# Softmax sums corrected on VectorE, weight sums in two jobs and weight conversion in another order, in a fused attention and two-layer MoE kernel

## The chip, the cores and the metric

One core of one Trainium2 chip. The metric is the device time of one execution in microseconds (us); the kernel before was timed three times and the median counts.

## The reference, cut to what matters

```python
attn = exp(scores - max);  attn = attn / (sum(attn) + 1e-09);  x = attn @ v     # window of 128, B=2, H=8, S=576, D=64
p = domain_probs / (domain_probs.sum(-1) + 1e-09)
for e in range(4):  out += p[:, e] * (relu(x @ w1[e]) @ w2[e])                  # x 1152x512, w1 512x1024
h = out @ w_in;  g = h * cos(h);  return g @ w_out                              # w_in 512x2048, in float64 words
```

## The kernel before

Every product of the two MoE stages is made in three TensorE passes over operands split into a high and a low part. The high part is a ScalarE (ACT) copy, the low part a subtraction on GpSimd (POOL) or VectorE (DVE). All subtractions are recorded under the helper's line, L130, so they are told apart by tile: `w1t` and `w2t` are split weights, `sm` sums of weight blocks, `xs` and `xq` split activations, `h` and `hpair` split hidden values.

The program order is written by hand. Each engine works through its own list in that order, and SyncE (SP) does the same with the DMAs it issues.

**Attention** (0 to 94 us) runs over 20 steps k, two for each block of queries, four heads in one step. Step k makes the scores and exponentials of k, the sums and reciprocals of step k-1 (`att_sums`), one weight job, the transposes of step k-3, the normalisation of step k-1 on POOL (`att_normalise`) and the product with v of step k-4 (after which `split_x` or `transformed` splits the result, ACT first and DVE behind it):

```python
at(k, att_scores); at(k - 1, att_sums); fill(k, 0)
at(k - LAG, att_transpose); at(k - 1, att_normalise); fill(k, 1)
at(k - LAG - 1, att_pv); fill(k, 2)
```

From k = 4 each `fill(k, 0)` takes one job from the generator `weights()`. A job is half a split (an ACT cast and a POOL subtraction), or the four POOL sums of `first_sums` in one go.

**Groups 0 to 7** (`early`) are the ReLU MoE, 512 hidden columns each; groups 8 to 11 are the cosine layer, whose weights `convert` makes from float64 words while groups 0 to 6 run (32 conversions of five stages, `cv`). A group is a list of steps made by `steps(g)`: two calls of `pair` (seven products over `xs`), `layer2(g, t)` for nine row tiles t (product over `h` for t < 3, over `hpair` otherwise) and `plain(g + 1, q)` (P0 to P3, a product of the next group over `xq`). `run` does for each step: the matmuls, then `advance` (one stage of every open cosine chain), the step's jobs, its `cv` stages, `move(2)` (two stages of a transform), and last the step's own evacuation. Group 7 (`turn`) also transposes the MoE's result by `flip(t)`, written f1 to f8, and builds the new operands `xs`.

The hidden values of a cosine group go through a chain of ACT, DVE, ACT, DVE, ACT, POOL, whose last instruction writes the low part in `hpair`.

Of the kernel before, what the change touches and what calls it, by code (L numbers as in the profile page):

```python
# [49 lines left out]
def tile_kernel(ctx, tc, qT, kT, v, probs, w1, w2, w_in, w_out, out):  # L50
    nc = tc.nc
# [96 lines left out]
    def weights():  # L148


        def two_parts(eng, hi, lo, src):
            n = src.shape[1] // 2
            for p in range(2):
                s = slice(p * n, (p + 1) * n)
                nc.scalar.activation(out=hi[:, s], in_=src[:, s], func=AF.Copy)  # L155
                sub(eng, lo[:, s], src[:, s], hi[:, s].bitcast(F32))
                yield

        raws = {}

        def first(g, j):
            raw = raws[j] = raw_t.pop((1, g, j))
            w = w_t[1, g, j] = w1p.tile([128, 2, 2, 1024], F32R, name="w1t", tag="w1t")
            yield from two_parts(nc.gpsimd, w[:, 0, 0], w[:, 1, 0], raw.rearrange("p m f -> p (m f)"))

        def first_sums(g, j):

            raw, w = raws[j], w_t[1, g, j]
            a11, a12 = raw[:, 0:2, 0:128], raw[:, 2:4, 0:128]
            a21, a22 = raw[:, 0:2, 128:256], raw[:, 2:4, 128:256]  # L170
            sm = ssp.tile([128, 4, 2, 128], F32, name="sm", tag="sm")
            nc.gpsimd.tensor_tensor(out=sm[:, 0], in0=a21, in1=a22, op=ALU.add)
            sub(nc.gpsimd, sm[:, 1], sm[:, 0], a11)
            sub(nc.gpsimd, sm[:, 2], a11, a21)
            sub(nc.gpsimd, sm[:, 3], a12, sm[:, 1])
            loads_ahead()
            yield
            yield from two_parts(nc.gpsimd, w[:, 0, 1], w[:, 1, 1], sm.rearrange("p s m f -> p (s m f)"))

        def second(g, j):  # L180
            raw = raw_t.pop((2, g, j))
            w = w_t[2, g, j] = w2p.tile([128, 2, 2, DM], F32R, name="w2t", tag="w2t")
            for f in range(2):
                nc.scalar.activation(out=w[:, 0, f], in_=raw[:, f], func=AF.Copy)  # L184
                sub(nc.gpsimd, w[:, 1, f], raw[:, f], w[:, 0, f].bitcast(F32))
                if f:
                    loads_ahead()
                yield

        for g in range(NG1 + NG2):  # L190
            for todo, j in order_of(g):
                yield from {"raw": first, "sums": first_sums, "second": second}[todo](g, j)
# [60 lines left out]
    def converts():  # L253

        gens = [convert(k) for k in range(32)]
        next(gens[0])
        for k, c in enumerate(gens):
            if k + 1 < len(gens):
                next(gens[k + 1])
            yield from c  # L260
# [72 lines left out]

    state, xps = {}, {}

    def att_scores(u, g):
        b, i = u
        s0, n = UNITS[i]
# [10 lines left out]
                )  # L349
        p = ppool.tile([128, 4, 256], F32, name="p", tag="p")  # L350
        nmax = stp.tile([128, 4], F32, name="nmax", tag="nmax")
        den = stp.tile([128, 4], F32, name="den", tag="den")
        rec = stp.tile([128, 4], F32, name="rec", tag="rec")
        for m in range(2):
            for hh in range(2):
                k = 2 * m + hh
                h = 4 * g + k
                nc.vector.tensor_tensor_reduce(  # L358
                    out=p[:n, k, :wid], in0=ps[hh][:n, m, :wid], in1=bm[:n, h, c0 : c0 + wid],
                    scale=-0.125, scalar=3.0e38, op0=ALU.add, op1=ALU.min,  # L360
                    accum_out=nmax[:n, k : k + 1],
                )
                nc.scalar.activation(  # L363
                    out=p[:n, k, :wid], in_=p[:n, k, :wid], func=AF.Exp, scale=-1.0,
                    bias=nmax[:n, k : k + 1], accum_out=den[:n, k : k + 1],
                )
        state[u, g] = p, den, rec, wid

    def att_sums(u, g):
        n = UNITS[u[1]][1]  # L370
        p, den, rec, wid = state[u, g]
        nc.gpsimd.tensor_scalar(out=den[:n], in0=den[:n], scalar1=1e-9, scalar2=None, op0=ALU.add)
        nc.vector.reciprocal(out=rec[:n], in_=den[:n])  # L373

    def att_normalise(u, g):
        n = UNITS[u[1]][1]
        p, den, rec, wid = state[u, g]
        for s in (slice(0, 2), slice(2, 4)):
            nc.gpsimd.tensor_tensor(  # L379
                out=p[:n, s, :wid], in0=p[:n, s, :wid],  # L380
                in1=rec[:n, s].unsqueeze(2).to_broadcast([n, 2, wid]), op=ALU.mult,
            )
        state[u, g] = p

# [293 lines left out]
    with tc.manual_schedule():  # L678

        warm = ppool.tile([128, 4, 256], F32, name="warm", tag="p")  # L680
        nc.vector.memset(warm[:, 0], 0.0)
        for _ in range(WARM):
            nc.tensor.matmul(
                ps1.tile([128, 512], F32, name="o_ps", tag="o_ps")[:, :256],
                warm[:, 0, :128], warm[:, 0], start=True, stop=True,
            )
# [4 lines left out]
        def fill(k, s):  # L691
# [4 lines left out]
                nc.sync.dma_start(out=pr, in_=probs.rearrange("(t p) e -> p t e", p=128))  # L696
            if (k, s) == (11, 0):
                routing()
            if s == 0 and 4 <= k < 18:
                next(jobs)  # L700
            if s == 1 and 12 <= k < 20:
                q, half = divmod(k - 12, 2)
# [23 lines left out]
    def steps(g):  # L726
# [15 lines left out]
            if turn and j == 0:  # L742
                yield flip(0), 0, 0, 0
        if g > 0:
            yield layer2(g, 1), 2, 2 * turn, 2
            yield layer2(g, 2), 2, 2 if turn else int(not last), 2
        order = (
            ("f1", 3, "f2", 6, "f3", "P0", "f6", 4, "P1", 7, "f4", 5, "f7", 8, "f5", "P2", "f8", "P3") if turn else
            ("P0", 6, 3, "P1", 7, 4, "P2", 8, "P3", 5)
        )  # L750
        njobs = 0 if last else 2 if turn else 5 if early else 9
        if g == 0:
            njobs += 1
        for k, o in enumerate(order):
            more = min(njobs, 2 if g == 0 and k == 0 else 1)
            if isinstance(o, int):
                assert not any(c > 0 for c, _ in chains)
                yield layer2(g, o), 2, more, 2 if k in (1, 4, 7) else 1 if k < 9 else 0
            elif o[0] == "f":
                yield flip(int(o[1])), 0, 0, 0  # L760
                continue
            elif not last:
                yield plain(g + 1, int(o[1])), 2, more, 2
            njobs -= more

    def run(groups):
        for g in groups:
            for step, stages, njobs, ncv in steps(g):
                next(step)
                for _ in range(stages):  # L770
                    advance()
                for _ in range(njobs):
                    next(jobs)
                for _ in range(ncv):
                    next(cv, None)
                move(2)
                next(step, None)
            while moved:
                move(24)
# [2 lines left out]
    hpair = hpp.tile([128, 2, NFG, PAIR], F32R, name="hpair")  # L782
    cv = converts()
    with tc.manual_schedule():
        run(range(NG1 - 1))
        left = sum(1 for _ in cv)
        assert not left, left
# [43 lines left out]
```

## Time and profile before

| | |
|---|---|
| Time, median of 3 (lowest, highest) | 676.09 us (674.96, 679.61) |
| The profiled execution: time, span of its instructions | 675.06 us, 673.3 us |
| TensorE busy (matmul, weight load) | 648.1 us, 569.5 us |
| VectorE, ScalarE, GpSimd busy | 420.4, 336.7, 372.4 us |

The span is the time from the first instruction to the last; the execution's own time is 1.8 us longer. Busy times of engines overlap. TensorE's idle time is in three places: the attention, the passage from group 0 to group 1 (130 to 146 us) and the turn (460 to 500 us). Between them the profile shows it busy without a break for 10-us slices on end.

### The profile page before, as it was taken

The numbers are of one execution on the slowest core, as the hardware profiler recorded it, in microseconds if no ns is written. First come the engines' busy times: TensorE is split into PE (matmuls) and PEld (weight loads), VectorE is DVE, ScalarE is ACT, GpSimd is POOL, SyncE is SP. The second block draws the span as 40 slices with busy tenths as digits, with TensorE's granted clock in tenths as the row PEclk, the third lists the DMA queues.
The fourth block names the chain that finished last, engine by engine and source line by source line (L and its number), as shares of the span: only waits on it lengthen the run. The fifth ranks groups of instructions, "written<-read, shape, count | busy, mean of one in ns | idle before, by whom it ended". The sixth has DMA issues, their size and how long they took to land.

```text
span 673.3 us, 9797 instructions
## 1 busy us (share of the span) xinstructions
PE 648.1 (96%) x3516; PEld 569.5 (85%) x3516; DVE 420.4 (62%) x821; ACT 336.7 (50%) x768; POOL 372.4 (55%) x376
## 2 busy tenths in 40 slices
PE   8879999979999999999999999999899999999997
PEld 5667789878898898998998998988788998998976
DVE  5645674587866858659669663455675464564562
ACT  6868744245334334344343251246675675675660
POOL 3987737517538147357166174194458749649540
PEclk7989999999999999999999999999999999999999
DMA  8135101553625504526325322011001200201002
GB/s 259 40 121 164 32 1 34 183 159 87 198 76 156 173 32 156 173 57 207 104 102 202 126 48 78 32 63 33 1 32 33 77 17 32 93 2 47 34 31 93
DMA packets 39728, 60.41 MB, mean 90 GB/s; under 512 B 5632, under 2 KB 22016, under 8 KB 39680
## 3 DMA queue, kind: packets, MB, share of 16 engines
q1 hardware_dynamic: 39680, 59.80, 27.7%
q8 instruction: 27, 0.44, 0.3%
q14 instruction: 21, 0.17, 0.1%
HBM read 49.04 MB, written 10.75 MB: 89 GB/s over the span
## 4 chain that ended last, share of the span: by engine, by line
PE 75%; DVE 8%; ACT 6%; POOL 5%; issue 3%; DMA 2%; SPq 0%; ACTq 0%; DVEq 0%; POOLq 0%
PE o_ps L627 38%; PE o_ps L533 20%; PE o_ps L561 13%; POOL p L379 2%; DVE u L505 2%; ACT r L503 2%; PE s_ps L346 2%; DMA cr<-w_in 2%; ACT u L502 2%; PE x_ps L429 2%; POOL hpair L130 1%; PE t_ps L401 1%; DVE o_ps L576 1%; DVE u L511 1%; DVE c L576 1%
## 5 line engine op out<-in xcount | busy, mean ns | idle before, releaser
L627 PE MATMUL o_ps<-w2t,hpair 128*128 128x512 f32 x864 | 207.2, 392 | 1.2 <-POOL hpair L130 1.0
L627 PEld LDWEIGHTS o_ps<-w2t,hpair 128*128 128x128 f32 x864 | 160.7, 188 | 35.1 <-POOL hpair L130 2.3
L533 PE MATMUL o_ps<-xs,w1t 128*128 128x384 f32 x1008 | 182.3, 336 | 8.3 <-ACT p L582 3.0
L533 PEld LDWEIGHTS o_ps<-xs,w1t 128*128 128x128 f32 x1008 | 175.4, 188 | 13.7 <-ACT p L582 3.9
L130 POOL TENSOR_TENSOR w1t<-raw,w1t 128x512 fp32r<-128x512 f32 x48 | 66.1, 1390 | 95.3 <-ACT w1t L155 95.2
L130 POOL TENSOR_TENSOR w2t<-raw,w2t 128x512 fp32r<-128x512 f32 x48 | 62.4, 1312 | 90.0 <-ACT w2t L184 88.7
L561 PE MATMUL o_ps<-xq,w1t 128*128 128x384 f32 x576 | 110.3, 338 | 0.0
L561 PEld LDWEIGHTS o_ps<-xq,w1t 128*128 128x128 f32 x576 | 101.6, 188 | 3.3
L627 PE MATMUL o_ps<-w2t,h 128*128 128x512 f32 x432 | 103.3, 392 | 0.0
L627 PEld LDWEIGHTS o_ps<-w2t,h 128*128 128x128 f32 x432 | 80.5, 188 | 16.1 <-issue 0.2
L505 DVE SCALAR_TENSOR_TENSOR u<-r,u 128x384 f32<-128x384 f32 x48 | 38.7, 810 | 57.8 <-ACT r L503 57.8
L130 POOL TENSOR_TENSOR w1t<-sm,w1t 128x512 fp32r<-128x512 f32 x48 | 67.2, 1416 | 7.4 <-ACT w1t L155 7.3
L130 POOL TENSOR_TENSOR hpair<-u,hpair 128x384 fp32r<-128x384 f32 x32 | 32.6, 1039 | 42.5 <-ACT hpair L513 42.5
L155 ACT ACTIVATE w1t<-sm 128x512 fp32r<-128x512 f32 x48 | 30.3, 631 | 45.7 <-POOL sm L130 45.7
L521 DVE SCALAR_TENSOR_TENSOR hpair<-o_ps,hpair 128x384 fp32r<-128x384 f32 x48 | 26.7, 556 | 33.1 <-ACT hpair L520 33.1
L363 ACT ACTIVATE p<-p,nmax 128x256 f32<-128x256 f32 (+2 forms) x80 | 36.3, 455 | 17.0 <-DVE nmax L358 17.0
L232 ACT ACTIVATE cr<-cr 128x512 int32<-128x512 uint32 x32 | 21.6, 675 | 44.6 <-DMA cr<-w_in 30.9
L520 ACT ACTIVATE hpair<-o_ps 128x384 fp32r<-128x384 f32 x48 | 23.4, 488 | 40.2 <-DVE o_ps L576 39.5
L244 ACT ACTIVATE cr<-cr 128x512 f32<-128x512 f32 x32 | 21.7, 679 | 38.9 <-DVE cv L238 38.9
L642 DVE SCALAR_TENSOR_TENSOR accpair<-o_ps,pr,accpair 128x512 f32<-128x512 f32 x42 | 31.0, 744 | 12.5 <-PE o_ps L627 12.5
L379 POOL TENSOR_TENSOR p<-p,rec 128x512 f32<-128x512 f32 (+2 forms) x40 | 34.1, 872 | 5.6 <-DVE rec L373 5.6
L234 DVE TENSOR_SCALAR cv<-cr 128x512 int32<-128x512 int32 x32 | 21.7, 678 | 24.6 <-DMA cr<-w_in 20.8
(99 smaller groups left out, 826.9 us busy)
## 6 DMA issues: line engine op xcount, KB each, us to landing
raw<-w SPq DMA_DIRECT2D x32, 512.0 KB, 3.9
cr<-w_in SPq DMA_DIRECT2D x16, 512.0 KB, 5.0
cr<-w_out SPq DMA_DIRECT2D x16, 512.0 KB, 4.2
wi<-cv SPq DMA_DIRECT2D x16, 256.0 KB, 4.4
wo<-cv SPq DMA_DIRECT2D x16, 256.0 KB, 2.3
raw<-wi SPq DMA_DIRECT2D x8, 512.0 KB, 3.4
raw<-wo SPq DMA_DIRECT2D x8, 512.0 KB, 3.6
qt<-qT SPq DMA_DIRECT2D x8, 256.0 KB, 4.3
```

The costliest lines, as they stand in the source:

```text
L130: eng.tensor_tensor(out=out, in0=a, in1=b, op=ALU.subtract)
L155: nc.scalar.activation(out=hi[:, s], in_=src[:, s], func=AF.Copy)
L234: nc.vector.tensor_scalar(out=o, in0=hw, scalar1=3, scalar2=0x3FFFFFF8, op0=ALU.logical_shift_left, op1=ALU.bitwise_and,)
L363: nc.scalar.activation(out=p[:n, k, :wid], in_=p[:n, k, :wid], func=AF.Exp, scale=-1.0, bias=nmax[:n, k : k + 1], accum_out=den[:n, k : k ...
L379: nc.gpsimd.tensor_tensor(out=p[:n, s, :wid], in0=p[:n, s, :wid], in1=rec[:n, s].unsqueeze(2).to_broadcast([n, 2, wid]), op=ALU.mult,)
L505: nc.vector.scalar_tensor_tensor(out=u, in0=r, scalar=MAGIC, in1=u, op0=ALU.subtract, op1=ALU.subtract)
L520: nc.scalar.activation(out=hi, in_=src, func=AF.Relu)
L521: nc.vector.scalar_tensor_tensor(out=lo, in0=src, scalar=0.0, in1=hi.bitcast(F32), op0=ALU.max, op1=ALU.subtract)
L533: nc.tensor.matmul(ps, w(a, k, m), xs[:, bb, b, m], start=(start and m == 0 and (a, bb) == PASSES[0]), stop=(stop and m == 1 and (a, bb) = ...
L561: nc.tensor.matmul(ps, w(a, 2 * (q % 2) + d // 2, d % 2), xq[:, bb, d], start=(d == 0 and (a, bb) == PASSES[0]), stop=(d == ND - 1 and (a, ...
L627: nc.tensor.matmul(ps, h0[:, a, f, t * 128 : (t + 1) * 128] if t < NQ else hpair[:, a, f, (t - NQ) * 128 : (t - NQ + 1) * 128], w_t[2, g, ...
L642: nc.vector.scalar_tensor_tensor(out=o, in0=ps, scalar=s, in1=o, op0=ALU.mult, op1=ALU.add)
```

## The change

- The sums of exponentials and the 1e-9 lie side by side in one tile, `dens` (four steps deep, filled with 1e-9 once). ScalarE's accumulator writes beside the constant. A VectorE reduction over the two replaces the GpSimd addition ahead of the reciprocal.
- The normalisation of the first batch element is one GpSimd instruction over four heads, not two over two heads each. The second batch element keeps two.
- `first_sums` hands back control after two of its four sums: a group's weights are 16 jobs, no longer 14. The attention gives 16 steps a job (k = 4 to 19), and the number of jobs in the steps of each group changes with it. The step `layer2(g, 1)` of groups 1 to 6 and 8 to 10 now holds one job.
- The first conversion's load is issued ahead of group 0. In the groups the `cv` stages stand in earlier steps (two in each of the first seven steps of `order`, then 1, 1, 0), the same number in all.
- `move(2)` comes before `advance`, the jobs and `cv`. In the turn P2 is cut in two halves, with f8 between them.

```diff
@@ first_sums
             sub(nc.gpsimd, sm[:, 1], sm[:, 0], a11)
+            yield
             sub(nc.gpsimd, sm[:, 2], a11, a21)
@@ converts
         next(gens[0])
+        yield
@@ att_scores, att_sums, att_normalise
-        den = stp.tile([128, 4], F32, name="den", tag="den")
+        den = dens[:, (2 * units.index(u) + g) % 4]
...
-                    bias=nmax[:n, k : k + 1], accum_out=den[:n, k : k + 1],
+                    bias=nmax[:n, k : k + 1], accum_out=den[:n, k, 0:1],
...
-        nc.gpsimd.tensor_scalar(out=den[:n], in0=den[:n], scalar1=1e-9, scalar2=None, op0=ALU.add)
-        nc.vector.reciprocal(out=rec[:n], in_=den[:n])
+        nc.vector.tensor_reduce(out=rec[:n], in_=den[:n], axis=mybir.AxisListType.X, op=ALU.add)
+        nc.vector.reciprocal(out=rec[:n], in_=rec[:n])
...
-        for s in (slice(0, 2), slice(2, 4)):
+        for s in (slice(0, 4),) if u[0] == 0 else (slice(0, 2), slice(2, 4)):
@@ fill
-            if s == 0 and 4 <= k < 18:
+            if s == 0 and 4 <= k < 20:
                 next(jobs)
@@ steps
-            yield layer2(g, 1), 2, 2 * turn, 2
+            yield layer2(g, 1), 2, 2 if turn else int(not last), 2
...
-            ("f1", 3, "f2", 6, "f3", "P0", "f6", 4, "P1", 7, "f4", 5, "f7", 8, "f5", "P2", "f8", "P3") if turn else
+            ("f1", 3, "f2", 6, "f3", "P0", "f6", 4, "P1", 7, "f4", 5, "f7", 8, "f5", "P2a", "f8", "P2b", "P3") if turn else
             ("P0", 6, 3, "P1", 7, 4, "P2", 8, "P3", 5)
...
-        njobs = 0 if last else 2 if turn else 5 if early else 9
+        njobs = 0 if last else 4 if turn else 6 if early else 10
         if g == 0:
-            njobs += 1
+            njobs += 2
...
-                yield layer2(g, o), 2, more, 2 if k in (1, 4, 7) else 1 if k < 9 else 0
+                yield layer2(g, o), 2, more, 2 if k < 7 else 1 if k < 9 else 0
...
+    def half(step, end):
+        next(step)
+        yield
+        if end:
+            whole(step)
@@ run
                 next(step)
+                move(2)
                 for _ in range(stages):
                     advance()
...
-                move(2)
                 next(step, None)
...
+        next(cv)
         run(range(NG1 - 1))
```

GpSimd in the attention, about steps 8 to 10. `p` are the exponentials (normalised here), `den` their sums. Before:

```order
L372 TENSOR_SCALAR den<-den 128x4
L172 TENSOR_TENSOR sm<-raw 128x256
L130 TENSOR_TENSOR sm<-sm,raw 128x256
L130 TENSOR_TENSOR sm<-raw 128x256
L130 TENSOR_TENSOR sm<-raw,sm 128x256
L379 TENSOR_TENSOR p<-p,rec 128x512 x2
```

and now:

```order
L172 TENSOR_TENSOR sm<-raw 128x256
L130 TENSOR_TENSOR sm<-sm,raw 128x256
L383 TENSOR_TENSOR p<-p,rec 128x1024
L130 TENSOR_TENSOR sm<-raw 128x256
L130 TENSOR_TENSOR sm<-raw,sm 128x256
```

The addition is gone, the normalisation is one instruction, and one stands between the two halves of the weight sums.

SyncE's DMAs at the start of the groups. `cr` are words to be converted, `raw` weights, `wi` converted weights written back. Before:

```order
L145 DMA raw<-w 128x4x256
L145 DMA raw<-w 128x2x512
L224 DMA cr<-w_in 128x1024 x2
L145 DMA raw<-w 128x4x256
L251 DMA wi_120<-cv 128x512
L224 DMA cr<-w_in 128x1024
```

and now:

```order
L225 DMA cr<-w_in 128x1024
L145 DMA raw<-w 128x4x256
L145 DMA raw<-w 128x2x512
L225 DMA cr<-w_in 128x1024
L252 DMA wi_120<-cv 128x512
L225 DMA cr<-w_in 128x1024
L145 DMA raw<-w 128x4x256
```

The first load of words stands ahead of two weight loads, and the first write-back and the third load of words stand ahead of the weight load that they followed.

GpSimd in cosine group 9 (10 has the same; 8 the same from the last four `hpair` on). Before:

```order
L130 TENSOR_TENSOR w1t<-raw,w1t 128x512
L130 TENSOR_TENSOR hpair<-u,hpair 128x384 x5
L130 TENSOR_TENSOR w1t<-raw,w1t 128x512 x2
L172 TENSOR_TENSOR sm<-raw 128x256
L130 TENSOR_TENSOR sm<-sm,raw 128x256
```

and now:

```order
L130 TENSOR_TENSOR w1t<-raw,w1t 128x512
L130 TENSOR_TENSOR hpair<-u,hpair 128x384 x3
L130 TENSOR_TENSOR w1t<-raw,w1t 128x512
L130 TENSOR_TENSOR hpair<-u,hpair 128x384 x2
L130 TENSOR_TENSOR w1t<-raw,w1t 128x512
L172 TENSOR_TENSOR sm<-raw 128x256
```

A weight subtraction has moved ahead of the last two of the group's eight `hpair` subtractions.

## Rows read from the trace of the kernel before

**Rows 1.** The page, busy time, share and count of each engine.
```profile
PE 648.1 (96%) x3516; PEld 569.5 (85%) x3516; DVE 420.4 (62%) x821; ACT 336.7 (50%) x768; POOL 372.4 (55%) x376
```

**Rows 2.** Timeline of POOL, attention: start, us, instruction, idle before and its releaser.
```profile
24.23 1.28 POOL L130 TENSOR_TENSOR w1t<-raw,w1t 128x512 fp32r<-128x512 f32 x1 [1.00 <-ACT w1t L155]
...
41.73 2.03 POOL L379 TENSOR_TENSOR p<-p,rec 128x512 f32<-128x512 f32 x2
43.84 0.21 POOL L372 TENSOR_SCALAR den<-den 64x4 f32<-64x4 f32 x1
```

**Rows 3.** Timeline of PE, attention.
```profile
46.46 0.63 PE L401 MATMUL t_ps<-ident,p 128*128 128x128 f32 x4 [1.08 <-POOL sm L130]
...
61.22 1.03 PE L401 MATMUL t_ps<-ident,p 128*64 128x128 f32 x8 [0.84 <-DVE pt L411]
...
79.97 1.09 PE L429 MATMUL x_ps<-pt,vt 128*64 128x128 f32 x16 [1.24 <-ACT xs L276]
```

**Rows 4.** Groups by form: busy us, mean ns, idle before and releasers.
```profile
L184 ACT ACTIVATE w2t<-raw 128x512 fp32r<-128x512 f32 x48 | 28.7, 623 | 0.0
...
L379 POOL TENSOR_TENSOR p<-p,rec 128x512 f32<-128x512 f32 x24 | 24.6, 1046 | 3.1 <-DVE rec L373 3.1
...
L379 POOL TENSOR_TENSOR p<-p,rec 128x384 f32<-128x384 f32 x8 | 6.4, 826 | 1.3 <-DVE rec L373 1.3
```

**Rows 5.** Timeline of DVE, attention.
```profile
44.09 0.17 DVE L373 RECIPROCAL rec<-den 64x4 f32<-64x4 f32 x1 [2.31 <-POOL den L372]
44.19 0.15 DVE L479 TENSOR_REDUCE prs<-pr 128x9 f32<-128x36 f32 x1
...
60.25 0.18 DVE L373 RECIPROCAL rec<-den 128x4 f32<-128x4 f32 x1 [2.21 <-POOL den L372]
```

**Rows 6.** The chain that ended last: start, us, what; groups 0 to 2.
```profile
116.51 4.76 DMA cr<-w_in
...
129.49 6.03 DMA cr<-w_in
...
146.43 9.44 PE o_ps L533 x54
...
186.26 5.22 PE o_ps L533 x30
```

**Rows 7.** Timeline of SP's queue.
```profile
128.46 0.38 SPq L145 DMA_DIRECT2D raw<-w  x1
```

**Rows 8.** Timeline of PE, end of group 0 and start of group 1.
```profile
133.95 2.27 PE L533 MATMUL o_ps<-xs,w1t 128*128 128x384 f32 x12
...
142.33 1.33 PE L533 MATMUL o_ps<-xs,w1t 128*128 128x384 f32 x6 [2.27 <-ACT p L582]
143.51 2.92 PE L627 MATMUL o_ps<-w2t,h 128*128 128x512 f32 x12
```

**Rows 9.** Timeline of DVE, group 2.
```profile
219.71 1.40 DVE L642 SCALAR_TENSOR_TENSOR accpair<-o_ps,pr,accpair 128x512 f32<-128x512 f32 x2
```

**Rows 10.** Timeline of PE, the turn.
```profile
479.70 5.98 PE L533 MATMUL o_ps<-xs,w1t 128*128 128x384 f32 x30 [2.04 <-ACT xs L276]
486.98 2.35 PE L533 MATMUL o_ps<-xs,w1t 128*128 128x384 f32 x12 [1.30 <-DVE c L576]
```

**Rows 11.** Timeline of ACT, the turn.
```profile
483.83 0.48 ACT L582 ACTIVATE p<-o_ps 128x384 f32<-128x384 f32 x1
```

**Rows 12.** Timeline of POOL, groups 8 and 9.
```profile
506.61 3.95 POOL L130 TENSOR_TENSOR hpair<-u,hpair 128x384 fp32r<-128x384 f32 x4 [5.20 <-ACT hpair L513]
...
555.44 3.99 POOL L130 TENSOR_TENSOR hpair<-u,hpair 128x384 fp32r<-128x384 f32 x4 [4.80 <-ACT hpair L513]
```

**Rows 13.** Timeline of PE, groups 8 and 9.
```profile
508.01 5.68 PE L627 MATMUL o_ps<-w2t,hpair 128*128 128x512 f32 x24
...
556.31 2.01 PE L627 MATMUL o_ps<-w2t,hpair 128*128 128x512 f32 x8
558.51 3.96 PE L627 MATMUL o_ps<-w2t,hpair 128*128 128x512 f32 x16 [0.19 <-POOL hpair L130]
```

More of the change, by code (lines that the diff above doesn't have):

```diff
@@ L334, in tile_kernel @@
     state, xps = {}, {}
+    dens = mkp.tile([128, 4, 4, 2], F32, name="dens")
     def att_scores(u, g):
@@ L377, in att_normalise @@
         p, den, rec, wid = state[u, g]
-        for s in (slice(0, 2), slice(2, 4)):
+        for s in (slice(0, 4),) if u[0] == 0 else (slice(0, 2), slice(2, 4)):
             nc.gpsimd.tensor_tensor(
                 out=p[:n, s, :wid], in0=p[:n, s, :wid],
-                in1=rec[:n, s].unsqueeze(2).to_broadcast([n, 2, wid]), op=ALU.mult,
+                in1=rec[:n, s].unsqueeze(2).to_broadcast([n, s.stop - s.start, wid]), op=ALU.mult,
             )
@@ L681, in tile_kernel @@
         nc.vector.memset(warm[:, 0], 0.0)
+        nc.vector.memset(dens, 1e-9)
         for _ in range(WARM):
@@ L744, in steps @@
         if g > 0:
-            yield layer2(g, 1), 2, 2 * turn, 2
+            yield layer2(g, 1), 2, 2 if turn else int(not last), 2
             yield layer2(g, 2), 2, 2 if turn else int(not last), 2
         order = (
-            ("f1", 3, "f2", 6, "f3", "P0", "f6", 4, "P1", 7, "f4", 5, "f7", 8, "f5", "P2", "f8", "P3") if turn else
+            ("f1", 3, "f2", 6, "f3", "P0", "f6", 4, "P1", 7, "f4", 5, "f7", 8, "f5", "P2a", "f8", "P2b", "P3") if turn else
             ("P0", 6, 3, "P1", 7, 4, "P2", 8, "P3", 5)
         )
-        njobs = 0 if last else 2 if turn else 5 if early else 9
+        njobs = 0 if last else 4 if turn else 6 if early else 10
         if g == 0:
-            njobs += 1
+            njobs += 2
         for k, o in enumerate(order):
-            more = min(njobs, 2 if g == 0 and k == 0 else 1)
+            more = min(njobs, 2 if g == 0 and k < 2 else 1)
             if isinstance(o, int):
                 assert not any(c > 0 for c, _ in chains)
-                yield layer2(g, o), 2, more, 2 if k in (1, 4, 7) else 1 if k < 9 else 0
+                yield layer2(g, o), 2, more, 2 if k < 7 else 1 if k < 9 else 0
             elif o[0] == "f":
@@ L762, in steps @@
             elif not last:
-                yield plain(g + 1, int(o[1])), 2, more, 2
-            njobs -= more
+                if len(o) < 3:
+                    yield plain(g + 1, int(o[1])), 2, more, 2 if k < 7 else 1
+                else:
+                    if o[2] == "a":
+                        halved = plain(g + 1, int(o[1]), True)
+                    yield half(halved, o[2] == "b"), 1, 0, 0
+            njobs -= more
+    def half(step, end):
[3 more added lines that the diff above has]
+            whole(step)
     def run(groups):
```

## Prediction

> **What bounds the kernel now.** I read the page first. TensorE (PE) is busy for 648.1 of 673.3 us [rows 1], so no edit can win more than the 25 us in which it is not, and an edit on another engine counts only where PE waits for it. The timeline of PE then shows where that is: in the attention, at the passage from group 0 to group 1, in the turn, and for a few tenths in each cosine group [rows 3, 8, 10, 13]. In groups 1 to 6 it has no gap. For each of the four places I went back along the chain of waits to the engine that sets it.
>
> In the first half of the attention it is POOL: normalisation, addition and weight job follow one another there with gaps of 0.08 us (43.76 to 43.84 [rows 2]), up to the transposes of step 9 at 46.46 [rows 3]. From then on it is PE. At the passage to group 1, ACT and DVE stand still in front of two loads of words [rows 6], fall behind with emptying PSUM, and PE runs out of banks [rows 8]. In the turn it is the transform and the cosine chains on ACT and DVE, in turns [rows 10, 11]. In the cosine groups the third `hpair` subtraction of the second pair is only just in time [rows 12, 13].
>
> **The change, part A, attention.** (1) POOL up to the end of the normalisation of step 9, which was at 41.73 + 2.03 = 43.76 us [rows 2]. Six additions (steps 3 to 8) lie in the busy stretch, each 0.22 with a gap of 0.08: 1.8 us less. Seven normalisations become one instruction each. From 384 to 512 elements one grows by 1046 - 826 = 220 ns, 1.72 ns an element [rows 4]; 1024 elements then take 1046 + 512 x 1.72 = 1.93 us against 2.03 for the two halves [rows 2]: 0.7 us less. Jobs 4 to 10 hold four splits, two halves of sums and one split; before they held one split more, 1.28 us [rows 2]. Against this stands the wait of POOL for ACT's cast at 24.23, 1.00 us [rows 2]: POOL will be there 0.9 us sooner, but the cast stands behind exponentials that ACT and DVE hand to each other at their own pace, so the wait grows by that much. 1.8 + 0.7 + 1.3 - 0.9 = 2.9 us.
>
> (2) From 43.76 to the transposes at 46.46 another 2.7 us pass: addition, reciprocal (DVE had waited 2.31 for it), the routing's four instructions and a PSUM copy stand in line on DVE [rows 3, 5]. Now the reciprocal waits for ACT alone, those follow it earlier, and PE waits for the normalisation itself: 2.6 us less. (3) The same chain made the 0.84 at 61.22, behind a reciprocal that waited 2.21 [rows 3, 5]: 0.8 less. (4) Jobs now also stand in steps 18 and 19. A cast of `w2t` (0.62, some 0.5 beside its neighbours [rows 4]) comes ahead of the transform for which PE waits 1.24 at 79.97 [rows 3]: 0.5 more. Their POOL halves hide beside PE.
>
> (5) Twenty reductions of about 0.15 us, by the nearest row, the routing's [rows 5], are 3 us on DVE, which waits for 2.2 and 2.3 at two single reciprocals; on the path they count once, 0.2 more. The fill of `dens` hides in DVE's first wait. Sum: -2.9 - 2.6 - 0.8 + 0.5 + 0.2 = -5.6; for handovers between engines that I left out I take **-5.3**. The ends: -2 (only the additions' own time) and -7 (the cast moves up too, and no handover costs anything).
>
> [...] The half of 512 elements took 1.02 us in the pair of 2.03 [rows 2]. [...]
>
> **Part B, conversion.** PE starts group 1 at 133.95 and its second block of 54 matmuls at 146.43 [rows 6, 8]. In between lie 30 matmuls (5.22 when nothing is in the way [rows 6]) and 12 wider ones (2.92 [rows 8]), 8.1 us; 146.43 - 133.95 - 8.1 = 4.4 us are lost. Their cause is the two loads at 116.51 and 129.49 [rows 6]: the first was issued only behind a weight load that waited for its buffer, the third stood behind another such load, at 128.46 [rows 7]. Now load 0 is issued ahead of group 0, and load 2 directly behind the first write-back. Load 1 still stands behind two weight loads and lands near 121. It is wanted in step "3", where ACT and DVE will stand until then, but with two steps and a whole conversion more behind them than before, so the delay at 121 us is three products and not five; eight banks hold that. Load 3 may hold them up by another 1.5. I take **-4.2**, with ends -2 (the second wait stays by half) and -4.4.
>
> **Part C, turn.** PE loses 2.04 at 479.70 (for the last transform) and 1.30 at 486.98 (for the sums of the pair) [rows 10]. With f8 ahead of half of P2 the last transform starts up to 1.05 us (6 of 12 matmuls) sooner, and with `move(2)` first no cosine stage stands in it: the 2.04 goes. What is late next is the copy at 483.83 [rows 11], behind the same transform; it comes some 1.5 sooner, so PE, 2 us sooner, waits longer there. **-1.5**; ends +0.5 (cosine chains late) and -3.3 (both waits go).
>
> **Part D, cosine groups.** The new job of `layer2(g, 1)` puts a `w1t` subtraction (1.28 [rows 2]) on POOL between the second and the third of the last four `hpair` subtractions. PE waits for the third: in group 9 these four start at 555.44, one each 1.0 us, and PE goes on at 558.51, after 8 of 12 matmuls [rows 12, 13]. The third now ends 1.25 later, and PE with it: 1.2 us. Group 10 repeats this. In group 8 the third ends at 509.6 and is wanted at 508.0 + 2.0 = 510.0 [rows 12, 13]: 0.9 us. Nothing hides it, because PE has no other work in line. **+3.3**; ends 0 (were the job to slip behind) and +4.2 (the cast, 0.5 on ACT, comes on top in two of three).
>
> **Part E, no cost.** In groups 1 to 6 conversion stages come up to two earlier. DVE empties two products together at 219.71 [rows 9], some 6 us behind PE; eight banks of about 2.4 us each leave over 10.
>
> Sum against the profiled execution: 675.06 - 5.3 - 4.2 - 1.5 + 3.3 = 667.4. The median of the runs is 1.0 above that execution, so the forecast for the median is **668.4 us**, 1.1% faster. One per cent, 6.8 us, is about what a measurement of this kernel can tell from no change.
>
> **Rivals.** *The hand-over of ACT and DVE bounds the attention.* Every second step ACT splits x, DVE follows, and only then come the next scores; this spoke in (1) already through the cast. If it paces every step, A falls to its end of -2: 671.7. For it: the wait at 24.23. Against: POOL had only that one gap. *The weight job in the cosine groups is hidden*, D = 0: 665.1; it needs the first two `hpair` subtractions 1.2 us earlier, and POOL waits for ACT there by 4.80 [rows 12]. *Loads 1 and 3 still cost half*, B = -2: 670.6. *Slower: DVE falls behind in groups 1 to 6.* With two stages more ahead of the emptying (some 3 us), its delay of 6 would become 9; from about 14 on PE runs out of banks. If each of the six groups then lost half of what group 0 lost, 2.2 us, the time is 668.4 + 13 = 681.4. Against it: with 6 us of delay PE has no gap in any of these groups.
>
> **How the numbers follow.** Forecast 0.56, ACT and DVE 0.20, job hidden 0.12, loads 0.08, DVE behind 0.04. The forecast's own spread is about 665 to 671 from the ends of A and C. The range that leaves no more than 2 in 10 out reaches over the first two rivals: 663.6 to 672.9. Faster by over 1% (below 669.3): three quarters of the forecast, all of "job hidden", a tenth of "ACT and DVE", a third of "loads": 0.42 + 0.12 + 0.02 + 0.03 = 0.59. Slower: 0.04. Within 1%: 0.37.
>
> **What would show it.** A: no reciprocal waits for POOL, the first `plain` product starts near 42 and the pair of group 0 near 89 us. B: no PE gap at the start of group 1. C: the 2.04 ahead of `xs` is gone, a longer wait two products on. D: PE waits of 1 to 1.5 us for `hpair` in groups 8, 9 and 10, three in all. Wrong would be: a POOL normalisation near 2.1 us with gaps for ACT at every step, or a `hpair` wait that doesn't grow.

## The result and the profile after

The changed kernel takes **670.79 us** (median of 8 runs, 668.29 to 672.44) against 676.14 (8 runs, 674.96 to 679.61): a ratio of 0.9907, with a 95% interval of 0.9885 to 0.9929. The forecast was 668.4. The runs after lie in two heaps, 668.3 to 669.8 and 671.7 to 672.4; the profiled execution, 668.45 with a span of 666.7, is of the lower one.

Line numbers of the changed kernel are 4 higher than before from L346 on (L376 is the new reduction, the addition L372 is gone). Part 1 of its page, with busy time, share of the span and instructions; PE is 2.5 us shorter busy than in [rows 1], DVE 12.4 longer, of which the reductions are only 20 x 0.16:

```profile
PE 645.6 (97%) x3516; PEld 568.7 (85%) x3516; DVE 432.8 (65%) x842; ACT 335.9 (50%) x768; POOL 367.6 (55%) x346
```

**Attention.** The timeline of PE, after (start, duration, what, the idle time before it and its releaser):

```profile
31.88 0.45 PE L350 MATMUL s_ps<-kt,qt 64*64 64x64 f32 x8
...
38.98 0.92 PE L350 MATMUL s_ps<-kt,qt 64*128 64x192 f32 x8 [0.78 <-DMA kt<-kT]
39.98 1.06 PE L405 MATMUL t_ps<-ident,p 128*128 128x128 f32 x8
...
54.05 1.06 PE L405 MATMUL t_ps<-ident,p 128*64 128x128 f32 x8
...
73.41 1.09 PE L433 MATMUL x_ps<-pt,vt 128*64 128x128 f32 x16 [1.48 <-ACT xs L278]
```

The first of these rows, the first scores of the second batch, before:

```profile
34.43 0.45 PE L346 MATMUL s_ps<-kt,qt 64*64 64x64 f32 x8
```

The transposes of step 9, whose second half waited until 46.46 in [rows 3], start at 39.98. The 0.84 is gone, the 1.24 of [rows 3] is 1.48. New is a wait for the load of `kt`. POOL in the same stretch:

```profile
22.65 1.27 POOL L130 TENSOR_TENSOR w1t<-raw,w1t 128x512 fp32r<-128x512 f32 x1 [1.10 <-ACT w1t L155]
23.88 1.89 POOL L383 TENSOR_TENSOR p<-p,rec 128x1024 f32<-128x1024 f32 x1
...
36.06 1.27 POOL L130 TENSOR_TENSOR w1t<-sm,w1t 128x512 fp32r<-128x512 f32 x1 [0.64 <-DVE nmax L362]
```

The merged normalisation takes 1.89 us; 1.93 was forecast. POOL now also waits for others.

**Passage to group 1.** SP's queue and PE, after:

```profile
85.57 0.34 SPq L225 DMA_DIRECT2D cr<-w_in  x1
104.89 6.02 SPq L145 DMA_DIRECT2D raw<-w  x2
110.96 0.46 SPq L225 DMA_DIRECT2D cr<-w_in  x1
112.79 0.34 SPq L252 DMA_DIRECT2D wi<-cv  x1
113.24 0.37 SPq L225 DMA_DIRECT2D cr<-w_in  x1
```
```profile
127.66 5.39 PE L537 MATMUL o_ps<-xs,w1t 128*128 128x384 f32 x30
135.64 9.55 PE L537 MATMUL o_ps<-xs,w1t 128*128 128x384 f32 x54
```

The first load of words stands ahead of the weight loads, the third right behind the first write-back. Group 1 has no gap; compare [rows 8].

**Turn and cosine groups.** PE after, in two stretches, and POOL in the second:

```profile
458.84 0.63 PE L660 MATMUL f_ps<-ident,accpair 128*128 128x128 f32 x4 [0.98 <-DVE accpair L646]
...
467.90 4.28 PE L537 MATMUL o_ps<-xs,w1t 128*128 128x384 f32 x23 [0.44 <-DVE xs L130]
473.88 1.32 PE L537 MATMUL o_ps<-xs,w1t 128*128 128x384 f32 x6 [1.69 <-ACT p L586]
476.50 3.91 PE L537 MATMUL o_ps<-xs,w1t 128*128 128x384 f32 x12 [1.31 <-DVE c L580]
...
500.56 3.96 PE L631 MATMUL o_ps<-w2t,hpair 128*128 128x512 f32 x16 [0.63 <-POOL hpair L130]
...
550.48 3.93 PE L631 MATMUL o_ps<-w2t,hpair 128*128 128x512 f32 x16 [1.37 <-POOL hpair L130]
```
```profile
546.21 2.03 POOL L130 TENSOR_TENSOR hpair<-u,hpair 128x384 fp32r<-128x384 f32 x2 [4.81 <-ACT hpair L517]
548.20 1.27 POOL L130 TENSOR_TENSOR w1t<-raw,w1t 128x512 fp32r<-128x512 f32 x1
549.44 2.30 POOL L130 TENSOR_TENSOR hpair<-u,hpair 128x384 fp32r<-128x384 f32 x2
```

The 2.04 of [rows 10] has shrunk to 0.44, but 1.69 stands behind it and the 1.30 is still there. The weight subtraction stands between the second and the third `hpair` subtraction, and PE waits.

**The balance by stages** comes from the starts of PE's blocks: the pair of group 0 (94.33 before, 88.19 after) and the blocks of 30 matmuls that open groups 2, 7, 9 and 11. Times in us between them; all kernels of the study are in it, and from group 2 to group 7 each takes 238.8, before and after, so part E cost nothing.

| kernel | pair 0 starts | to group 2 | 7 to 9 (turn, group 8) | 9 to 11 | to the end |
|---|---|---|---|---|---|
| before | 94.33 | 91.76 | 105.96 | 97.51 | 44.94 |
| changed | 88.19 | 87.23 | 107.46 | 99.80 | 45.22 |
| e0 changed, again | 92.65 | 87.22 | 107.42 | 99.86 | 45.15 |
| e1 job back | 88.87 | 87.23 | 107.47 | 97.37 | 45.26 |
| e2 turn back | 90.78 | 87.23 | 109.88 | 99.77 | 44.84 |
| e3 load back | 89.96 | 88.58 | 107.46 | 99.78 | 45.12 |
| e5 turn's jobs earlier | 94.53 | 87.22 | 104.78 | 97.40 | 45.17 |
| e6 and loads earlier | 90.56 | 87.22 | 104.78 | 97.42 | 45.22 |
| e7 stages back | 89.75 | 87.23 | 107.39 | 99.84 | 45.19 |
| e8 addition on POOL | 94.03 | 87.23 | 107.67 | 99.77 | 44.80 |
| e9 two halves | 88.30 | 87.23 | 107.29 | 99.79 | 44.89 |
| e10 one job | 91.08 | 87.40 | 105.17 | 97.48 | 44.87 |
| e11 one job, loads earlier | 90.93 | 87.42 | 104.89 | 97.49 | 44.87 |

So the change gives 6.1 us in this attention and 4.5 at group 1, and takes 1.5 back in the turn with group 8 and 2.3 in groups 9 and 10. Between the two executions of one program, changed and e0, only the first column differs; from group 0 on they agree within 0.1 us, and kernels that share a stage's program agree in it within some 0.4 us.

Of the 6.1 us, 2.55 lie ahead of the first scores of the second batch (34.43 before, 31.88 after) and 3.59 behind them (59.90 us from there to pair 0 before, 56.31 after).

### The profile page after: what moved, and what is told of

It is laid out like the page before. It is cut to its first block, busy times and chain, and to the rows that moved or that the text cites. A ratio compares the mean times of both kernels' runs of the same rounds, so it can differ in the third digit from the quotient of the medians.

```text
span 666.7 us, 9755 instructions
## 1 busy us (share of the span) xinstructions
PE 645.6 (97%) x3516; PEld 568.7 (85%) x3516; DVE 432.8 (65%) x842; ACT 335.9 (50%) x768; POOL 367.6 (55%) x346
## 4 chain that ended last, share of the span: by engine, by line
PE 78%; DVE 7%; ACT 7%; POOL 4%; issue 2%; DMA 1%; SPq 0%; ACTq 0%; DVEq 0%; POOLq 0%
PE o_ps L631 39%; PE o_ps L537 21%; PE o_ps L565 13%; PE s_ps L350 2%; DVE u L509 2%; ACT r L507 2%; ACT u L506 2%; PE x_ps L433 1%; POOL p L383 1%; POOL w1t L130 1%; PE t_ps L405 1%; POOL hpair L130 1%; DVE o_ps L580 1%; DVE xs L130 1%; DVE u L515 1%
## 5 line engine op out<-in xcount | busy, mean ns | idle before, releaser
L130 POOL TENSOR_TENSOR w2t<-raw,w2t 128x512 fp32r<-128x512 f32 x48 | 66.2, 1394 | 82.1 <-ACT w2t L185 82.1
L130 POOL TENSOR_TENSOR w1t<-sm,w1t 128x512 fp32r<-128x512 f32 x48 | 64.6, 1356 | 41.9 <-ACT w1t L155 35.1
L509 DVE SCALAR_TENSOR_TENSOR u<-r,u 128x384 f32<-128x384 f32 x48 | 34.6, 726 | 51.7 <-ACT r L507 51.7
L383 POOL TENSOR_TENSOR p<-p,rec 128x512 f32<-128x512 f32 (+5 forms) x30 | 32.6, 1102 | 9.5 <-DVE rec L377 5.6
L239 DVE SCALAR_TENSOR_TENSOR cv<-cr,cv 128x512 int32<-128x512 int32 x32 | 35.1, 1097 | 1.1
```

The lines of the kernel that those rows point to most:

```text
L130: eng.tensor_tensor(out=out, in0=a, in1=b, op=ALU.subtract)
L239: nc.vector.scalar_tensor_tensor(out=a, in0=hw, scalar=-0x40000000, in1=o, op0=ALU.bitwise_and, op1=ALU.bitwise_or,)
L383: nc.gpsimd.tensor_tensor(out=p[:n, s, :wid], in0=p[:n, s, :wid], in1=rec[:n, s].unsqueeze(2).to_broadcast([n, s.stop - s.start, wid]), op ...
L509: nc.vector.scalar_tensor_tensor(out=u, in0=r, scalar=MAGIC, in1=u, op0=ALU.subtract, op1=ALU.subtract)
```

## The experiments

Each was timed in 4 to 12 runs beside the kernel before. The edits are to the changed kernel, or to the experiment that is named.

### e0: the changed kernel again

> The changed kernel once more, unaltered, as the base for the others of this series. The first eight runs lay at 668.3 to 668.5 (three), 669.8 (one) and 671.7 to 672.4 (four). If that is only noise, five more fill the gap between. If the program really has two courses, they fall on the two heaps again, and a profile from the upper heap differs from the first one in one place by about 3.5 us. I expect the second, in the attention or at the passage to group 1, where loads decide (the load of kt at 34.55 took 4.30 us in the first profile); a rival is that the difference is spread over the whole span like a clock.

670.23 us (667.09 to 672.92), ratio 0.9906 (0.9880 to 0.9933): the same heaps. The profile caught the upper one, and it differs in one place only, the attention (92.65 against 88.19). PE in e0:

```profile
41.97 1.35 PE L350 MATMUL s_ps<-kt,qt 64*128 64x192 f32 x8 [2.56 <-DMA kt<-kT]
```

The wait for `kt` is 2.56 instead of 0.78. The other part of the difference lies earlier: the first scores of the second batch start at 33.09 instead of 31.88. So the difference lies in the attention and is not spread over the span. That the attention has just two courses is not shown: the seven traces of kernels with this attention (changed, e0, e1, e2, e3, e5, e7) start pair 0 at 88.19 to 94.53, with no two neighbours more than 1.9 us apart.

### e1: the job of the cosine groups back

```
-yield layer2(g, 1), 2, 2 if turn else int(not last), 2
+yield layer2(g, 1), 2, 2 if turn else int(early), 2
-njobs = ... 6 if early else 10
+njobs = ... 6 if early else 11      # the first step takes two
```

> The changed kernel, but in the cosine groups no weight job stands in layer2(g, 1); the job comes one step later and the first step after it takes two. Theory: the w1t subtraction (1.29 us) that now stands between the second and the third hpair subtraction makes PE's waits for hpair (0.63, 1.37, 1.4 us, together 4.1 in 4 places against 1.0 in 3 before). It goes: PE's waits for hpair fall to about 1.0 in sum, groups 9 and 10 take 48.7 us each again instead of 49.9, and the time falls by 3.0 us against the unaltered changed kernel. Rival: PE waits there because the cosine chains of ACT come later; then the waits stay and the time is the same.

666.27 us (665.80 to 669.09), ratio 0.9865 (0.9845 to 0.9885). POOL in group 9 of e1, after the same wait as above:

```profile
546.89 3.98 POOL L130 TENSOR_TENSOR hpair<-u,hpair 128x384 fp32r<-128x384 f32 x4 [4.80 <-ACT hpair L517]
```

The four subtractions stand together again, PE's waits for `hpair` in groups 9 and 10 fall to 0.17 each (0.19 and 0.17 before), and 9 to 11 takes 97.37, as before the change. By the trace that is 2.4 us. The median fell by 4.0 against e0; the rest is probably the attention, which the medians mix in. In group 8 the 0.63 went too, but the stretch stayed at 107.47. PE's granted clock was 0.64 on the mean there from 477 to 485 us, against 0.79 in the same stretch of the first profile. That need not be the reason: in e0 the clock of this stretch was 1.00, and it took 107.42 all the same, with waits of 0.70 for `p` and 0.99 for `hpair`. So what the job in group 8 costs on balance is not shown.

### e2: the turn back

```
-"f5", "P2a", "f8", "P2b", "P3"
+"f5", "P2", "f8", "P3"
     (and move(2) behind jobs and conversions again)
```

> The changed kernel with the turn as before: P2 in one piece, f8 behind it, and move(2) behind jobs and conversions. In the first profile of the changed kernel the stretch from the start of the last ReLU group to that of group 9 took 107.5 us against 106.0 before, of which the job of layer2(8, 1) explains 0.6. Theory: the last transform was not made earlier, because it has to wait for the transform of f7 to end and then runs at the pace at which ACT and DVE hand over to each other; the 2.04 us in front of xs have only become waits for p and c behind it (1.69, 1.31 and some 1.5 in pieces). Undone, the 2.04 comes back and those shrink: 0.8 us faster. Rival, my prediction: the new order is worth 1.5 us; then this is 1.5 us slower.

672.98 us (669.92 to 673.94), ratio 0.9948 (0.9928 to 0.9968). My theory fell: undone, the turn takes 109.88, which is 2.4 more than with the new order, and 3.9 more than before the change, although this order is the one from before. What differs is the weight jobs. The split sums make 16 jobs of 14 for each group, and in the turn the two more go to the end of the line (group 8 has one more as well, whose price e1 left open). ACT, POOL and DVE in e2, one row each:

```profile
452.97 0.62 ACT L155 ACTIVATE w1t<-sm 128x512 fp32r<-128x512 f32 x1
```
```profile
453.66 1.30 POOL L130 TENSOR_TENSOR w1t<-sm,w1t 128x512 fp32r<-128x512 f32 x1 [4.02 <-ACT w1t L155]
```
```profile
453.92 1.31 DVE L130 TENSOR_TENSOR xs<-accpair,xs 128x256 fp32r<-128x256 f32 x1 [1.42 <-ACT xs L278]
```

The last cast and its subtraction stand inside the first `accpair` transform. Before the change they were done by then. The `xs` subtraction on DVE takes 1.31 beside POOL's, against 0.42 for most of its kind. The delay is handed on, and PE pays at f7:

```profile
462.36 0.83 PE L660 MATMUL f_ps<-ident,accpair 128*128 128x128 f32 x4 [1.91 <-DVE accpair L646]
462.85 4.48 PE L631 MATMUL o_ps<-w2t,hpair 128*128 128x512 f32 x12
```

In the other kernels the 12 matmuls take 3.0; here the granted clock from 458 to 466 us is 0.79 on the mean, against 1.00 before the change.

### e3 and e7: the two halves of the conversion edit

e3 takes the load ahead of group 0 away, e7 the new distribution of the stages:

```
e3: -next(gens[0]); yield      -next(cv) ahead of run()
e7: -layer2(g, o), ... more, 2 if k < 7 else 1 if k < 9 else 0
    +layer2(g, o), ... more, 2 if k in (1, 4, 7) else 1 if k < 9 else 0
    -plain(g + 1, ...), ... more, 2 if k < 7 else 1
    +plain(g + 1, ...), ... more, 2
```

> The changed kernel without the load of words ahead of group 0 (the first next(cv) and the yield behind it are gone); the distribution of the conversion stages stays. Theory: the load ahead is what closed the gap of 4.5 us at the passage to group 1, since the first two loads then stand behind weight loads on SP's queue again. ACT and DVE stop in front of them, PE runs out of banks early in group 1, and the time rises by 4 us. Rival: it is the other distribution of the stages in group 0 that closed the gap; then the time is the same, within 1 us.

> The changed kernel with the distribution of the conversion stages behind layer2 and plain as before; the load ahead of group 0 stays. With that load taken away, PE lost 1.35 us at the start of group 1 of the 4.5 that it lost before the change. Theory: most of the gain there, some 3 us, is from the earlier stages; then this run loses about 3 us in group 1, with PE waits like those before the change. Rival, my prediction: the load ahead does it alone, and this run loses 1.5 us or less.

e3: 672.96 us (669.92 to 677.27), ratio 0.9955 (0.9933 to 0.9978). e7: 670.33 us (669.47 to 676.44), ratio 0.9932 (0.9908 to 0.9957). The stage column decides. Without the load ahead, 1.35 us of the 4.5 come back (88.58), although ACT stands 7.7 us in front of the first words; without the new distribution nothing comes back (87.23). The theory of e3 (4 us) was too large, that of e7 (3 us) fell and its rival held. Either edit alone removes most of the gap, so neither can be credited with the whole, and what they give can't be added.

One thing both leave in place. The third load of words stood behind a weight load before (129.49 behind 128.46 [rows 6, 7]), and stands ahead of the next weight load in e3 (120.74 and 125.32 in SP's queue) and in e7 (114.77 and 118.57), as in the changed kernel. ACT's wait for it, before and in e3 (in e7 there is none):

```profile
135.60 0.68 ACT L232 ACTIVATE cr<-cr 128x512 int32<-128x512 uint32 x1 [6.51 <-DMA cr<-w_in]
```
```profile
124.74 0.68 ACT L233 ACTIVATE cr<-cr 128x512 int32<-128x512 uint32 x1 [0.29 <-DMA cr<-w_in]
```

That would explain why one edit is nearly enough; a run that moves this load alone was not made.

### e5: the turn's jobs earlier

As e1, and in the turn:

```
-yield layer2(g, 1), 2, 2 if turn ...     -yield layer2(g, 2), 2, 2 if turn ...
+yield layer2(g, 1), 2, 3 if turn ...     +yield layer2(g, 2), 2, 3 if turn ...
-njobs = 0 if last else 4 if turn ...
+njobs = 0 if last else 2 if turn ...
```

> The changed kernel with the job of layer2(g, 1) taken back in the cosine groups, as in the run before, and in the turn the two jobs that the split sums add put earlier: layer2(7, 1) and layer2(7, 2) take three each, so that the last cast of w1t no longer stands in the transforms. In the run with the old turn, this cast (452.97) and its subtraction on POOL stood between the stages of the second transform, PE waited 1.91 for f7 where it had waited 0.48, and the next 12 matmuls took 4.48 instead of 3.00. Theory: the split of the sums costs 2 to 3 us in the turn in this way and the new order of the turn hides most of it; with the jobs earlier the stretch from the last ReLU group to group 9, 107.5 us in both, falls to about 105, and the time by 2 us against the run with the job taken back (666.3). Rival: the last transform's own chain sets the turn in any case; then the stretch stays at 107 us.

665.54 us (663.39 to 670.27), ratio 0.9860 (0.9824 to 0.9896). The stretch falls to 104.78, 2.7 less than in e1, and the wait for f7 is gone. PE in e5:

```profile
472.87 4.29 PE L537 MATMUL o_ps<-xs,w1t 128*128 128x384 f32 x23 [0.21 <-DVE xs L130]
478.84 1.32 PE L537 MATMUL o_ps<-xs,w1t 128*128 128x384 f32 x6 [1.69 <-ACT p L586]
481.47 2.38 PE L537 MATMUL o_ps<-xs,w1t 128*128 128x384 f32 x12 [1.30 <-DVE c L580]
```

This is the new turn without the late casts: the 2.04 of [rows 10] down to 0.21, a wait of 1.69 two products on, the 1.30 unchanged. Against before it is worth 1.2 us. The median shows only 0.7 against e1; the runs are spread over 7 us, and the profiled one (span 667.9) has the latest pair 0 of the table. PE in its attention, and windows with busy us and instructions of PE, PEld, DVE, ACT, POOL, then granted clock, DMA share and GB/s:

```profile
42.72 1.65 PE L350 MATMUL s_ps<-kt,qt 64*128 64x192 f32 x8 [2.84 <-DMA kt<-kT]
45.92 2.27 PE L565 MATMUL o_ps<-xq,w1t 128*128 128x384 f32 x6
```
```profile
40.00:44.00 4.00, 1.28 (x8) 1.17 (x8) 1.84 (x3) 1.12 (x3) 3.92 (x6) 0.73 0.78 269
44.00:48.00 4.00, 4.00 (x18) 3.38 (x14) 2.01 (x11) 2.35 (x9) 2.18 (x5) 0.50 0.02 7
```

PE idles for 2.84 us, and its granted clock reads 0.73 from 40 to 44 us and 0.50 from 44 to 48, against 1.00 in both windows of the changed kernel: the six matmuls that take 1.30 there take 2.27 here. Here the late load costs more than its wait: the wait is 2.06 longer than in the changed kernel, and from the first scores with `kt` to pair 0 it is 60.97 us against 56.31, 4.66 longer.

### e6: the units' loads earlier

```
-load_units_to(k // 2 + 2)
+load_units_to(k // 2 + (3 if k >= 8 else 2))     # on e5
```

> The kernel of the run before, and from step 8 of the attention on the loads of a unit (qt, kt, vt) are issued one unit ahead of where they stand now. In the traces of the changed kernel PE waits 0.78, 2.56, 0.75, 0.77 and 2.00 us for kt at about 39 us: that load is queued on SP behind a weight load that waits until POOL has ended the sums at 33.5. Theory: this load is what now bounds the attention where POOL did before; with it out of the way the wait of 0.8 to 2.6 goes and the attention ends 1 to 2 us sooner, more in the executions that lay high. Rival: the normalisation on POOL is late next and takes most of it back; then 0.3 us or less.

665.96 us (665.82 to 668.40), ratio 0.9862 (0.9837 to 0.9887). The wait for `kt` is gone, and PE waits for something else, right behind it:

```profile
42.35 1.06 PE L405 MATMUL t_ps<-ident,p 128*128 128x128 f32 x8 [0.93 <-DVE pt L415]
```

From the first scores with `kt` to pair 0 it is 56.31 us, exactly as in the executions whose `kt` came 0.75 to 0.78 late (changed, e1, e7, 56.30 in e2). With 2.00 late it is 59.00 (e3), with 2.56 59.56 (e0), with 2.84 60.97 (e5). So a `kt` that is a little late costs nothing, because another chain, through DVE's copy, ends at the same time, and a late one costs 2.7 to 4.7. The median didn't gain, as the rival had it, though what is late next is that copy and not the normalisation on POOL. The runs lie closer together, but the low ones went with the high ones (665.82 to 668.40, in e5 663.39 to 670.27); five and six runs show no more than that.

### e8: the addition on POOL again

```
-nc.vector.tensor_reduce(out=rec[:n], in_=den[:n], axis=X, op=ALU.add)
-nc.vector.reciprocal(out=rec[:n], in_=rec[:n])
+nc.gpsimd.tensor_scalar(out=den[:n, :, 0], in0=den[:n, :, 0], scalar1=1e-9, op0=ALU.add)
+nc.vector.reciprocal(out=rec[:n], in_=den[:n, :, 0])
```

> The changed kernel with the addition of 1e-9 as an instruction of POOL again, ahead of the reciprocal, in place of the reduction on VectorE; the merged normalisation and all else stay. My prediction gave this edit about 1.8 us of POOL time, 2.6 us for the chain of addition, reciprocal, routing and copy at 43.8, and 0.8 us at 61 us: the first group's pair of products then starts some 4 to 5 us later than in the changed kernel (88.2 to 92.7 there, with the clock's course in the first 30 us). Rival: DVE's 20 reductions cost what the additions on POOL did, and PE is bound by the load of kt anyway; then the pair starts within 1 us of the same place.

673.47 us (671.38 to 674.29), ratio 0.9965 (0.9950 to 0.9980): more than half of the gain is gone. Pair 0 starts at 94.03, and from the first scores with `kt` it takes 59.37 instead of 56.31, with `kt` 1.42 late. Ahead of these scores, e6 can be set beside it: PE's rows agree within 0.1 us up to 21 us, and then the scores start at 34.25 in e6 and at 34.66 here. DVE and PE in e8:

```profile
58.96 0.18 DVE L377 RECIPROCAL rec<-dens 128x4 f32<-128x4 f32 x1 [2.03 <-POOL dens L376]
59.05 0.73 DVE L415 COPY pt<-t_ps 64x256 f32<-64x256 f32 x2
```
```profile
36.41 1.07 PE L405 MATMUL t_ps<-ident,p 128*128 128x128 f32 x8 [1.30 <-POOL sm L130]
...
59.93 1.03 PE L405 MATMUL t_ps<-ident,p 128*64 128x128 f32 x8 [0.83 <-DVE pt L415]
```

The 0.84 of [rows 3] is back at its place, with the reciprocal that waits for POOL and the copy behind it. POOL, whose rows follow one another with gaps under 0.1 us from 26 to 45 us, paces this stretch again. In sum the addition costs 3.5 us, less than the 4 to 5 expected.

### e9: normalisation in two halves

```
-for s in (slice(0, 4),) if u[0] == 0 else (slice(0, 2), slice(2, 4)):
+for s in (slice(0, 2), slice(2, 4)):
```

> The changed kernel with the normalisations of the first batch in two halves again; all else stays. My prediction gave the merging 0.7 us at the end of the ninth step (seven times 2.03 against 1.93; the merged instruction took 1.89 in the trace after). Theory: POOL reaches the sums some 0.6 us later, the weight load behind them and with it the load of kt move by as much, and the attention ends up to 1 us later; against executions of the same course the time rises by 0.5 to 1 us, which may not show in the medians. [...]

670.06 us (668.07 to 670.85), ratio 0.9914 (0.9888 to 0.9939). The pairs of halves take 2.03 to 2.04 against 1.89. Where the first scores with `kt` start at the same time (31.89 and 31.88), pair 0 starts at 88.30 against 88.19. The merging is worth 0.14 us on POOL each time and 0.1 us in all.

### e10 and e11: the sums in one job

e10 takes the second `yield` out of `first_sums` and counts the jobs as before (`4 <= k < 18`, `2 * turn` behind `layer2(g, 1)`, njobs 2, 5 and 9). e11 adds the earlier loads of e6.

> The changed kernel with the weight sums in one job again and the jobs of each step counted as before (none in steps 18 and 19 of the attention, two fewer in the turn, none in layer2(g, 1) of the cosine groups). Addition on VectorE, merged normalisation, conversion order and the new turn stay. Theory: the split gained nothing that the others do not give, and cost 2.7 us in the turn and 3 us in the cosine groups; without it the stretch from the last ReLU group to group 9 is 104.8 us and the groups 9 and 10 take 48.7 each. In the attention the sums are done a step earlier, and so the weight load behind them and the load of kt; the wait of 0.8 to 2.8 us for kt shrinks, while the normalisation of the ninth step comes 1.3 us later. In sum 5 to 6 us faster than the changed kernel, 664 to 666. Rival: the split is what made the attention shorter, and the attention loses 3 us or more of its gain; then 668.

> The kernel of the run before, and from step 8 of the attention on the loads of a unit are issued one unit earlier. Theory: where the sums are one job, the weight load that kt stands behind comes free earlier anyway, so that this gains little at the median (0 to 1 us) and only takes away the executions in which the load of kt is late. Rival: the load still bounds the attention, and it is 1 to 2 us faster than the run before.

e10: 665.96 us (664.44 to 672.23), ratio 0.9869 (0.9832 to 0.9907). e11: 665.66 us (664.28 to 666.22), ratio 0.9851 (0.9830 to 0.9871). Turn and cosine groups are those of e5 within 0.4 us. In the attention PE waits for POOL once more. PE in e10:

```profile
35.91 1.09 PE L404 MATMUL t_ps<-ident,p 128*128 128x128 f32 x8 [1.25 <-POOL p L382]
39.00 1.09 PE L404 MATMUL t_ps<-ident,p 128*128 128x128 f32 x8 [0.59 <-POOL p L382]
42.84 1.06 PE L404 MATMUL t_ps<-ident,p 128*128 128x128 f32 x8 [0.87 <-POOL sm L172]
...
50.23 1.14 PE L349 MATMUL s_ps<-kt,qt 64*128 64x256 f32 x8 [0.91 <-DMA kt<-kT]
```

From the first scores with `kt` to pair 0 it is 56.87 in e10, 0.6 more than in the changed kernel, but that is the last row. e11 has the same three waits for POOL (1.24, 0.59, 0.89), runs like e10 up to the product ahead of that row, doesn't wait for `kt` and takes 56.15. What the split gives and takes is read from e6 and e11, which both have the earlier loads. PE in e6, then in e11:

```profile
71.86 1.09 PE L433 MATMUL x_ps<-pt,vt 128*64 128x128 f32 x16
...
75.78 1.09 PE L433 MATMUL x_ps<-pt,vt 128*64 128x128 f32 x16 [1.47 <-ACT xs L278]
```
```profile
73.18 1.09 PE L432 MATMUL x_ps<-pt,vt 128*64 128x128 f32 x16
...
76.59 1.09 PE L432 MATMUL x_ps<-pt,vt 128*64 128x128 f32 x16 [1.29 <-ACT xs L277]
```

Counted from the first scores with `kt` (34.25 and 34.78), e6 with the split is 0.79 us ahead at the first of the two rows, 0.28 at the second, and 0.16 behind at pair 0. The split wins 0.8 us where POOL is waited for, and loses it again about the jobs that it brings into steps 18 and 19 (ACT casts `w2t` at 68.27 and 72.44 us in e6, and not in this stretch of e11).

So the change without its split is some 4 to 5 us better than with it, and e11, the steadiest, stands 1.5% below the kernel before. e5, e6, e10 and e11 can't be told apart by their medians.

## Why the prediction came out as it did

The time fell into the range, 2.4 us above the forecast, and 2.1 of these are the stretch of part C with group 8. The step that failed is **part C**, which put the price of the split sums in the turn at nothing.

**A, -5.3: near as a sum, in part by luck.** The profiled execution gives -6.1, e0 -1.7. At the median it is about -4.9: -5.35 between the medians, less the other four columns (-4.53, +1.50, +2.29, +0.28). The forecast had no term for what separates the two: the start of the first scores with `kt` (30.96 to 34.78 us in the traces after the change, 34.43 before) and the lateness of that load. The largest terms were those of the addition (1.8, 2.6 and 0.8, less 0.2 on DVE). e8 shows them real and smaller: 3.1 us behind the first scores with `kt`, the 0.8 among them, and 0.4 ahead of them. Inside (1) the sizes were off. The merging was worth 0.1 and not 0.7. The split was to win 1.3 and to lose 0.5 by term (4); it won 0.8 and lost that again (e6 and e11). Why these came to nothing: after the additions left, POOL was no longer the only one that PE waits for, and e10 and e11 wait for it without being later at pair 0 for it. What is late next I had not asked at this place. It is the load of `kt` where that comes late, in line on SP behind a weight load that POOL's sums release, and otherwise DVE's copy (e6).

The length of the merged instruction itself was near: the line through the rows of 384 and 512 elements [rows 4] gave 1.93 us for 1024, and all six merged normalisations took 1.89, 0.04 less.

**B, -4.2: -4.5.** The gap is gone, as forecast. That the load ahead alone would do is shown by e7; that the stages alone would have done 3.2 of it, by e3, I had not considered.

**C, -1.5: the wrong sign.** Forecast for the stretch with group 8 was -1.5 + 0.9, measured +1.5. The step read "With f8 ahead of half of P2 the last transform starts up to 1.05 us (6 of 12 matmuls) sooner, and with `move(2)` first no cosine stage stands in it: the 2.04 goes", and this came true where nothing else interferes: 2.04 to 0.21, a new wait two products on, -1.2 in sum (e5; -0.8 and -1.1 in e10 and e11, whose jobs in the turn stand as before the change). Missing was the price of the split in the turn. I had followed the two more jobs into the attention and the cosine groups, but not into the turn, where `njobs` goes from 2 to 4 and the last cast lands in the transforms; that is 2.3 to 2.7 us with the new order (e1 against e10, e11 and e5), and more with the old one (e2).

**D, +3.3: +2.3, and group 8 open.** Groups 9 and 10 took 2.3 more (2.4 forecast), and e1 shows the cause. PE waited 0.63 in group 8, and 0.99 in e0 (0.9 forecast), but without that job the stretch is no shorter (e1).

**E: as forecast.** 238.8 us for groups 2 to 6, before and after. Of the rivals, ACT and DVE did not bound the attention (pair 0 would start near 92 in every execution), D was not hidden, loads 1 and 3 did not keep half of B, DVE did not fall behind.

## What to carry to other kernels

When a step of a schedule that counts jobs is split, every later place in that count moves: follow the last job of each stage, not only the first. When an engine stops being the bound, its next savings can be worth next to nothing (here the merging, 0.14 us on POOL each time and 0.1 in all, e9) until the new bound is named, and that may be a load standing in a queue behind another that waits. Two cures for one gap should be tried apart before their gains are added.

## What was not expected

**The clock and the heaps.** While the first loads arrive, from 6 to 14 us, the granted clock of PE is 0.61 to 0.94 on the mean in nine of the thirteen traces, and 1.00 in the other four. In the changed kernel it is 1.00 from 6 to 8 us and 0.50 from 10 to 12. It comes back at a different time. Windows of the changed kernel, then of e2, which has the same program up to there:

```profile
14.00:22.00 8.00, 7.08 (x63) 4.64 (x62) 5.65 (x30) 7.17 (x29) 5.78 (x4) 1.00 0.62 155
```
```profile
14.00:22.00 8.00, 8.00 (x39) 5.86 (x40) 4.80 (x27) 6.16 (x23) 5.58 (x4) 0.50 0.61 150
```

A granted clock of 1.00 in one, 0.50 in the other, and 2.6 us between them at the first scores with `kt` (31.88 and 34.48). The clock's column alone doesn't tell the course: it reads 1.00 from 6 to 22 us in e3, e6, e8 and e10, but the same transposes take 1.06 in e3 and 1.91 in e6, as long as in e2 at 0.50. PE in e3, then in e6:

```profile
17.62 1.06 PE L404 MATMUL t_ps<-ident,p 128*64 128x128 f32 x8 [0.55 <-POOL p L382]
```
```profile
17.04 1.91 PE L405 MATMUL t_ps<-ident,p 128*64 128x128 f32 x8
```

Why the load of `kt` takes 4.3 us in one execution and some 6 in another (issued at 34.55 and 36.02, the scores behind it start at 38.98 and 41.97) stays open, as does what decides when the clock comes back.

**DVE beside POOL.** The 1.31 us for a subtraction that otherwise takes 0.42 (e2) ends 0.27 after POOL's, which had started 0.26 earlier. Most of DVE's 12.4 us more lie in two instructions of the conversion, 32 of each: the one at L239 takes 35.1 us in all, before (L238) 29.6, the one at L243 30.2, before (L242) 24.5. Their lengths differ by whether POOL is at work. At L239 the 14 with no POOL instruction beside them take 0.69 to 0.70 us each, and 16 of the other 18 take 1.11 to 1.76; before, 21 take 0.69 and the 11 beside POOL 1.10 to 1.75. No run was made that tells whether POOL holds them up.
